# Convolution and ELU layer on one core: x cast once per super through a DRAM copy, convolutions moved amid output rounds, loads reordered at the start

## Chip, cores, metric

One core of one Trainium2 chip. The metric is the device time of one execution in microseconds (us), lower is better. Executions of one kernel on one chip usually agree within a per cent (four of the kernel before: 850.81 to 853.84 us); a run more than 1.5% above the fastest of its kernel is called slow, the others fast. Ratios are computed as the mean time of one kernel's fast runs over that of the other's of the same rounds, so not quite the ratio of the medians quoted. Runs came from different chips, where the kernel before took 849 to 855 us; each run is therefore judged against the kernel before on its own chip.

## The reference

A softmax-weighted causal convolution over 7 tokens, 8 heads of 24 channels, then a two-layer network with ELU:

```python
# x (8, 4096, 192), weight (8, 7), w_in (192, 2048), w_out (2048, 192), all float32
w = softmax(weight, axis=-1)
att[b, s, h*24 + c] = sum_k w[h, k] * x_padded[b, s + k, h*24 + c]   # 6 zero rows in front
h = att.reshape(32768, 192) @ w_in
g = where(h > 0, h, exp(min(h, 0)) - 1)
out = g @ w_out                                                      # (32768, 192) float32
```

## The kernel before

The 32,768 tokens are worked off in 32 *supers* of 1,024. A super has 16 *steps*; in each, a pair of 64-row slices of h goes round a loop of four engines through one of three PSUM slots `H`:

```python
# TensorE (PE): 12 matmuls fill H[slot]; then 9 or 10 "output rounds" of g @ w_out
# ScalarE (ACT):   E = exp(H[slot])                         (2 x 512 columns)
# GpSimd (POOL):   E = max(min(E, 1), 0)                    "clamp"
# VectorE (DVE):   g = max(E - 1, H[slot])                  frees the slot
```

The convolution is also done by PE, in two parts per super, each of which takes one of the three slots; ScalarE evacuates it to `csb`, and it goes through DRAM (`conv_slots`) into `att` with another layout. x is cast from float32 to bfloat16 on its way into `xg`, in overlapping windows of 122 rows, and GpSimd issues these loads between its clamps:

```python
CONV_AT = ((7, 2, 0), (15, 2, 1))   # (step, supers ahead, part): after the rounds of steps 7 and 15
X_AT = (1, 5, 13)                   # steps at which GpSimd issues the x loads
...
for n in range(NP):                 # GpSimd's loop
    s, i = divmod(n, NQ)
    if i in X_AT and s + NXB < NS:
        load_x(s + NXB, X_AT.index(i))      # part 0: only where a batch begins; parts 1, 2: windows
    for u in range(2):
        W(s_exp, 2 * n + u + 1)
        g.tensor_scalar(out=E[:, n % NE, u, :], ..., op0=ALU.min, op1=ALU.max).then_inc(s_clp)
...
if n in rounds_at:                  # PE's order of work
    order.append(("o",) + rounds_at[n])
for at, ahead, g in CONV_AT:
    if i == at and s + ahead < NS and n < NP:
        conv_at(s + ahead, g)
```

After 64 output rounds the output is evacuated (`osb<-ops`, L271) twice per super, at steps 2 and 10. The distance between two such evacuations is called a *half* below; it is the pulse by which the text measures the loop.

## Time and profile before

| | before |
|---|---|
| median, three runs | 852.95 us |
| first output evacuation | 66.73 us |
| half, steady | 12.44 us |
| busy: PE, GpSimd, ScalarE, VectorE | 89, 78, 77, 76% |

The first and fourth parts of the page of the kernel before: busy time of each engine, and the chain of work that ended last, by engine. PEld is PE's loading of weights, which overlaps its matmuls (752.5 and 560.4 us of busy time in a span of 849.9).

```profile
PE 752.5 (89%) x25088; PEld 560.4 (66%) x25088; DVE 643.3 (76%) x1031; ACT 650.5 (77%) x1156; POOL 662.8 (78%) x1115
...
PE 35%; POOL 26%; DVE 17%; ACT 9%; issue 9%; DMA 3%; SPq 0%; POOLq 0%; ACTq 0%
```

No engine is full, the chain is mixed, and the engines wait for each other in a ring (80 to 770 us: VectorE for GpSimd 134.2 us, GpSimd for ScalarE 122.6, ScalarE for PE 100.7, PE for VectorE 30.7): so I read that the loop's latency through three slots bounds it. The next fence is that chain in order of time (start, length, what), in one half of the kernel before.

```profile
409.35 2.35 POOL E L248 x4
411.70 0.73 POOL xg L198
412.43 0.03 issue
412.46 0.64 POOL E L248
413.10 0.02 issue
413.13 2.49 DVE gT L333 x4
415.62 0.14 issue
415.75 0.37 PE H L392
```

The GpSimd issue of an x load (L198) stands between clamps, and everything behind it waits. What a part costs can be read from the run itself, because the x loads stop first and the convolutions next. This is the busy time of each engine in three stretches of the kernel before, each from one evacuation to the next: with convolution and x load, with convolution alone, with neither.

```profile
core 0: us, PE busy (x) PEld busy (x) DVE busy (x) ACT busy (x) POOL busy (x), PEclk, DMA share, GB/s
420.49:432.93 12.44, 11.64 (x400) 8.50 (x392) 10.09 (x17) 10.17 (x20) 10.24 (x18) 1.00 0.54 134
785.38:797.10 11.72, 11.63 (x396) 9.18 (x392) 10.01 (x17) 10.00 (x20) 9.46 (x17) 1.00 0.20 61
819.30:830.10 10.80, 10.78 (x360) 7.97 (x352) 10.01 (x17) 9.07 (x18) 9.45 (x17) 1.00 0.13 41
```

These are the lines of the waits of the kernel before that have PE waiting for *issue*, that is, for nothing the profile shows, between 80 and 770 us (total us, times, longest), and the line of the DMA queues that carries instructions.

```profile
PE ops L414 <- issue: 4.6, 4, 1.7
PE H L370 <- issue: 1.6, 1, 1.6
PE H L392 <- issue: 0.6, 1, 0.6
```

```profile
q8 instruction: 196, 3.21, 1.6%
```

The three waits sum to 6.8 us. The sum of these three lines is called *issue waits* below. The queue line says that instructions are fetched during the run: 196 packets, 3.21 MB. Each packet has 16,384 bytes in the trace's records. PE ran 25,088 matmuls and 25,088 weight loads (and 71 semaphore and drain instructions), 50,176 in all without the 71, which is 256 for each of the 196 packets. So I take these packets to be essentially PE's program (an estimate from these counts), one about every 4 us (3.98 in the median between 80 and 770 us).

### The profile page before, as it was taken

The page shows a single profiled execution, that of the slowest core. Times are in us where ns is not written, and L with a number is a line of the kernel's source. Part 1 is how long each engine was busy: PE and PEld are TensorE (multiplying, and loading weights), DVE is VectorE, ACT ScalarE, POOL GpSimd, SP SyncE. Part 2 cuts the span into 40 slices and gives each one's busy share as a digit, 9 for nine tenths or more (in the row PEclk, how much of TensorE's full clock was granted, in tenths as well). Part 3 has the DMA queues.
Part 4 walks back from the last instruction along what each step waited for, and adds up shares of the span by engine and source line. Part 5 has one row for each costly group of instructions (what it writes and reads, how often), then busy time and mean ns, then how long its engine had stood idle before and what let it go on. Part 6 is the DMA issues. An engine that isn't in the chain of part 4 may idle for free.

```text
span 849.9 us, 54707 instructions
## 1 busy us (share of the span) xinstructions
PE 752.5 (89%) x25088; PEld 560.4 (66%) x25088; DVE 643.3 (76%) x1031; ACT 650.5 (77%) x1156; POOL 662.8 (78%) x1115
## 2 busy tenths in 40 slices
PE   0279999889999999989999989999999999999997
PEld 0147667667766666766766766767766766677776
DVE  1277878777878878778777877878787887888894
ACT  1278888778878878878888868888787887888884
POOL 3378888778788788878788868788778878877883
PEclk9999999999999999999999999999999999999999
DMA  7774453444453444444335444344445434443211
GB/s 121 131 148 114 105 121 94 94 99 111 106 123 90 109 94 110 115 106 111 102 80 117 112 101 110 96 93 112 106 106 122 100 91 103 111 115 94 91 41 59
DMA packets 109190, 88.51 MB, mean 104 GB/s; under 512 B 46432, under 2 KB 95584, under 8 KB 108896
## 3 DMA queue, kind: packets, MB, share of 16 engines
q1 hardware_dynamic: 68016, 69.30, 26.1%
q0 software_dynamic: 40944, 15.72, 17.1%
q8 instruction: 196, 3.21, 1.6%
q14 instruction: 34, 0.28, 0.1%
HBM read 56.89 MB, written 42.24 MB: 117 GB/s over the span
## 4 chain that ended last, share of the span: by engine, by line
PE 35%; POOL 26%; DVE 17%; ACT 9%; issue 9%; DMA 3%; SPq 0%; POOLq 0%; ACTq 0%
POOL E L248 20%; PE H L392 19%; DVE gT L333 17%; PE ops L414 16%; ACT E L294 6%; POOL xg L198 5%; ACT osb L271 3%; DMA conv_slots<-csb 1%; DMA conv_band<-wprb 1%; DMA att<-conv_slots 1%; PE H L370 1%; DMA Tm<-conv_band 0%; SPq L475 0%; DMA wq<-in_weight_dram 0%; ACT csb L283 0%
## 5 line engine op out<-in xcount | busy, mean ns | idle before, releaser
L333 DVE SCALAR_TENSOR_TENSOR gT<-E,H 128x512 f16<-128x512 f32 x1024 | 640.0, 682 | 191.0 <-POOL E L248 182.1
L248 POOL TENSOR_SCALAR E<-E 128x512 f32<-128x512 f32 x1024 | 602.4, 614 | 148.1 <-ACT E L294 142.7
L294 ACT ACTIVATE E<-H 128x512 f32<-128x512 f32 x1024 | 546.6, 605 | 138.4 <-PE H L392 138.1
L392 PE MATMUL H<-att,w_in 64*64 64x512 bf16 x6144 | 429.7, 381 | 57.7 <-DVE gT L333 38.3
L414 PEld LDWEIGHTS ops<-w_out,gT 64*64 64x64 f16 x16384 | 377.9, 107 | 90.1 <-issue 9.5
L414 PE MATMUL ops<-w_out,gT 64*64 64x192 f16 x16384 | 422.5, 243 | 7.5 <-issue 6.4
L392 PEld LDWEIGHTS H<-att,w_in 64*64 64x64 bf16 x6144 | 165.9, 107 | 154.2 <-DVE gT L333 63.5
L283 ACT ACTIVATE csb<-H 128x1024 bf16<-128x1024 f32 x64 | 65.5, 1024 | 47.1 <-PE H L370 47.1
L370 PE MATMUL H<-Tm,xg 128*24 128x122 bf16 (+1 forms) x2560 | 43.2, 212 | 28.3 <-DMA Tm<-conv_band 15.2
L370 PEld LDWEIGHTS H<-Tm,xg 128*24 128x24 bf16 x2560 | 33.9, 93 | 41.2 <-DMA Tm<-conv_band 15.2
L198 POOL DMA_DIRECT2D xg<-in_x_dram x64 | 53.0, 830 | 10.2 <-DMA Tm<-conv_band 10.2
L271 ACT ACTIVATE osb<-ops 128x768 f32<-128x768 f32 x64 | 52.3, 817 | 8.4 <-PE ops L414 8.4
L235 POOL DMA_DIRECT2D w_out<-in_moe_w_out_dram x1 | 1.1, 1102 | 15.4 <-DMA att<-conv_slots 15.4
L207 POOL DMA_DIRECT2D xg<-in_x_dram x8 | 4.8, 604 | 0.3 <-issue 0.3
L217 POOL DMA_DIRECT2D w_in<-in_moe_w_in_dram x6 | 3.5, 606 | 0.3 <-PE H L370 0.3
L206 POOL MEMSET xg<- 6x192 bf16 x8 | 2.0, 247 | 0.3 <-POOLq L512 0.3
L326 DVE MEMSET H<- 128x2048 f32 x1 | 1.8, 1765 | 0.4 <-issue 0.4
L307 DVE TENSOR_REDUCE wmx<-wq 128x8 f32<-128x56 f32 x1 | 0.2, 213 | 2.2 <-DMA wq<-in_weight_dram 2.2
L260 ACT ACT_TABLE_LOAD x1 | 1.3, 1283 | 0.7 <-PEq L512 0.7
L264 ACT ACTIVATE wex<-wq 128x56 f32<-128x56 f32 x1 | 0.2, 249 | 1.7 <-DVE wq L309 1.7
L305 DVE MEMSET Tm<- 128x544 uint32 x1 | 0.5, 512 | 0.9 <-PEq L512 0.9
L316 DVE TENSOR_REDUCE wsum<-wex 128x8 f32<-128x56 f32 x1 | 0.2, 211 | 0.3 <-ACT wex L264 0.3
(9 smaller groups left out, 1.5 us busy)
## 6 DMA issues: line engine op xcount, KB each, us to landing
att<-conv_slots SPq DMA_DIRECT2D x192, 128.0 KB
out_dram<-osb SPq DMA_DIRECT2D x128, 192.0 KB, 3.3
conv_slots<-csb SPq DMA_DIRECT2D x64, 256.0 KB, 2.2
xg<-in_x_dram POOLq DMA_DIRECT2D x40, 192.0 KB, 3.7
xg<-in_x_dram POOLq DMA_DIRECT2D x24, 240.0 KB, 5.3
w_in<-in_moe_w_in_dram POOLq DMA_DIRECT2D x6, 128.0 KB, 5.6
w_in<-w_in SPq DMA_DIRECT2D x2, 384.0 KB, 5.3
w_out<-in_moe_w_out_dram POOLq DMA_DIRECT2D x1, 768.0 KB, 8.4
```

What stands on the lines that cost most here:

```text
L198: g.dma_start(xg[:, s % NXB, w0:w1, :], src).then_inc(s_x[s % NXB], 16)
L206: g.memset(xg[0:PAD, b, 0, :], 0.0).then_inc(s_z)
L207: g.dma_start(xg[PAD:P, b, 0, :], x_flat[t0 : t0 + P - PAD, :]).then_inc(s_x[b], 16)
L217: g.dma_start(w_in[0:HP, j, FH * k : FH * (k + 1)], bass.AP(tensor=moe_w_in.tensor, offset=8 * j * FF + FH * k, ap=[[CPH * FF, HEADS], [FF ...
L248: g.tensor_scalar(out=E[:, n % NE, u, :], in0=E[:, n % NE, u, :], scalar1=1.0, scalar2=0.0, op0=ALU.min, op1=ALU.max,).then_inc(s_clp)
L271: a.activation(osb[:, b, :, :, :].rearrange("p g k d -> p g (k d)"), ops[:, :, 0 : 2 * D], ACT.Copy,).then_inc(s_oev)
L283: a.activation(csb[:, m % 4, :, :], H[:, slot_of_conv[m] % 3, :].rearrange("p (b t) -> p b t", b=2), ACT.Copy,).then_inc(s_ce)
L294: a.activation(E[:, n % NE, u, :], H[:, k, GS * u : GS * (u + 1)], ACT.Exp).then_inc(s_exp)
L333: v.scalar_tensor_tensor(out=gT[:, s % NG3, 2 * q + u, :], in0=E[:, n % NE, u, :], scalar=1.0, in1=H[:, slot_of_pair[n] % 3, GS * u : GS * ...
L370: ins = pe.matmul(H[SLOT * q : SLOT * q + CPH, k % 3, GS * hb + o : GS * hb + o + nc_], xg[:, s % NXB, w, CPH * h : CPH * (h + 1)], Tm[:, ...
L392: ins = pe.matmul(H[HP * c : HP * (c + 1), k % 3, GS * r : GS * (r + 1)], w_in[HP * r : HP * (r + 1), j, HP * f : HP * (f + 1)], att[HP * ...
L414: ins = pe.matmul(ops[HP * c : HP * (c + 1), g, D * kb : D * (kb + 1)], gT[HP * g : HP * (g + 1), t % NG3, f, t0 : t0 + HP], w_out[HP * g ...
```

## The change

Its intent: leave GpSimd one DMA per super. GpSimd casts a whole super of x into a padded DRAM copy, four supers ahead; the windows are then plain loads from that copy, issued by SP. Convolutions go into the middle of the output rounds at steps 0 and 8. At the start, later loads are held back until the first `att` has landed, the att reads are shared between two queues, and idle matmuls are meant to keep PE's clock up.

```diff
+QA = 10
+WARM = (20, 18)
-CONV_AT = ((7, 2, 0), (15, 2, 1))
-X_AT = (1, 5, 13)
+CONV_AT = ((0, 2, 0), (8, 2, 1))
+EARLY_CONV = {5: (1, 0), 7: (1, 1), 11: (2, 0), 14: (2, 1)}
+CAST_AT, CAST_AHEAD = 2, 4
+LOAD_AT, LOAD_AHEAD = 4, 3
 ...                                                     # PE's order of work
+            t, half, r0, r1 = rounds_at[n]
+            mid = (r0 + r1) // 2 if convs else r1
+            order.append(("o", t, half, r0, mid))
+            for k, g in convs:
+                conv_at(k, g)
+            if mid < r1:
+                order.append(("o", t, half, mid, r1))
 ...                                                     # GpSimd, before its loop
             load_w_in(0)                                # now after the diagonal write
-            W(s_cv, 2)
+            W(s_att[0], 16 * NDMA_ATT)
+            if NS > 1:
+                load_x(1)
             load_w_in(1)
             ... w_out ...
+            if NS > 2:
+                load_x(2)
 ...                                                     # GpSimd's loop
-                if i in X_AT and s + NXB < NS:
-                    load_x(s + NXB, X_AT.index(i))
+                if i == CAST_AT and s + CAST_AHEAD < NS:
+                    k = s + CAST_AHEAD
+                    b, row = k // SPB, PAD + k % SPB * SUP
+                    g.dma_start(
+                        xpad[b, row : row + SUP, :].rearrange("(p k) d -> p (k d)", p=P),
+                        x_flat[k * SUP : (k + 1) * SUP, :].rearrange(
+                            "(p k) d -> p (k d)", p=P
+                        ),
+                    ).then_inc(s_xc[k % CAST_AHEAD], 16)
 ...                                                     # PE
+            warm(WARM[0])
 ...                                                     # the second warm-up, ScalarE's att reads
 ...                                                     # SP
-                    if s == 0:
-                        copy_w(1)
-                        copy_w(2)
+                    if m == 1:
+                        read_att(sy, W, 0, (0,))
+                        ...
+                        copy_w(1)
+                    elif m == 3:
+                        read_att(sy, W, 1, (0, 1))
+                        copy_w(2)
+                elif item[0] == "h":
+                    s, i = divmod(item[1], NQ)
+                    if i == 1 and s >= 1 and s + 1 < NS:
+                        W(s_h, NQ * s)
+                        read_att(sy, W, s + 1, (0, 1))
+                    k = s + LOAD_AHEAD
+                    if i == LOAD_AT and CAST_AHEAD <= k < NS:
+                        ...                              # waits for the casts
+                        x_windows(sy, xpad, k, 0, XW, row, s_xh)
+                        x_windows(sy, xpad, k, XW, NWIN, ..., s_xh)
```

More of the change, by code (lines that the diff above doesn't have):

```diff
@@ L102, in bass_lightweight_conv__then__act_elu_kernel @@
             order.append(("h", n))
-        if n in rounds_at:
-            order.append(("o",) + rounds_at[n])
-        for at, ahead, g in CONV_AT:
-            if i == at and s + ahead < NS and n < NP:
-                conv_at(s + ahead, g)
-        if n in (3, 5) and NS > 1:
-            conv_at(1, (3, 5).index(n))
+        if s == 0:
+            convs = [EARLY_CONV[n]] if n in EARLY_CONV else []
+        else:
+            convs = [(s + ahead, g) for at, ahead, g in CONV_AT if at == i and n < NP]
+        convs = [(k, g) for k, g in convs if k < NS]
+        if n in rounds_at:
+            t, half, r0, r1 = rounds_at[n]
[5 more added lines that the diff above has]
+                order.append(("o", t, half, mid, r1))
+        else:
+            for k, g in convs:
+                conv_at(k, g)
+    xpad = nc.dram_tensor("x_padded", (Bsz, PAD + S, D), BF16).ap()
     band = nc.dram_tensor("conv_band", (P, HEADS, TW), BF16).ap()
@@ L140, in bass_lightweight_conv__then__act_elu_kernel @@
         wprb = sbuf("wprb", [P, HEADS, KSIZE], BF16)
+        zrow = sbuf("zrow", [Bsz, PAD * D], BF16)
+        zw = sbuf("zw", [P, GS], BF16)
         scr = sbuf("scr", [P, 2], FP32)
@@ L152, in bass_lightweight_conv__then__act_elu_kernel @@
         s_z = sema("s_z")
+        s_zr = sema("s_zr")
+        s_zw = sema("s_zw")
+        s_zp = sema("s_zp")
+        s_xh = [sema(f"s_xh{i}") for i in range(NXB)]
+        s_xc = [sema(f"s_xc{i}") for i in range(CAST_AHEAD)]
         s_h = sema("s_h")
@@ L178, in __call__, with x_windows, read_att @@
                     self.eng.wait_ge(sem, value)
-        FH = FF // 2
+        WCOLS = ((0, P * QA), (P * QA, FF))
         NDMA_ATT = 6
-        x_need, x_count, z_count = {}, [0] * NXB, 0
+        x_need, x_count = {}, {}
         for s in range(NS):
-            x_count[s % NXB] += 32 + 16 * (s % SPB == 0)
-            z_count += s % SPB == 0
-            x_need[s] = (x_count[s % NXB], z_count)
+            sem = (s_x if s < CAST_AHEAD else s_xh)[s % NXB]
+            x_count[id(sem)] = x_count.get(id(sem), 0) + 32 + 16 * (s == 0)
+            x_need[s] = (sem, x_count[id(sem)])
+        def x_windows(eng, flat, s, w0, w1, row, sem):
+            src = bass.AP(
+                tensor=flat.tensor,
+                offset=row * D,
+                ap=[[D, P], [CW * D, w1 - w0], [1, D]],
+            )
+            eng.dma_start(xg[:, s % NXB, w0:w1, :], src).then_inc(sem[s % NXB], 16)
+        def read_att(eng, W, s, halves):
+            for m in (2 * s, 2 * s + 1):
+                W(s_dw[m % 4], 16 * (m // 4 + 1))
+            for r in halves:
+                for j in range(3):
+                    src = bass.AP(
+                        tensor=bounce.tensor,
+                        offset=(2 * P * (s % 2) + 8 * j) * SUP,
+                        ap=[[SLOT * SUP, HEADS], [SUP, 8], [1, SUP]],
+                    )
+                    eng.dma_start(
+                        att[HP * r : HP * (r + 1), s % 2, j, :, :].rearrange(
+                            "p g t -> p (g t)"
+                        ),
+                        src,
+                    ).then_inc(s_att[s % 2], 16)
         @block.gpsimd
@@ L190, in _gpsimd, with load_x @@
             W = Waits(g)
-            def x_windows(s, w0, w1, row):
-                src = bass.AP(
-                    tensor=x_flat.tensor,
-                    offset=row * D,
-                    ap=[[D, P], [CW * D, w1 - w0], [1, D]],
-                )
-                g.dma_start(xg[:, s % NXB, w0:w1, :], src).then_inc(s_x[s % NXB], 16)
-            def load_x(s, part):
+            def load_x(s):
                 b, t0 = s % NXB, s * SUP
-                first = s % SPB == 0
                 if s >= NXB:
                     W(s_cv, 2 * (s - NXB) + 2)
-                if part == 0 and first:
+                if s == 0:
                     g.memset(xg[0:PAD, b, 0, :], 0.0).then_inc(s_z)
@@ L209, in load_x @@
                     ).then_inc(s_x[b], 16)
-                elif part == 1:
-                    x_windows(s, int(first), XW, t0 - PAD + CW * first)
-                elif part == 2:
-                    x_windows(s, XW, NWIN, t0 + SUP - P - CW * (NWIN - 1 - XW))
+                w0 = int(s == 0)
+                x_windows(g, x_flat, s, w0, XW, t0 - PAD + CW * w0, s_x)
+                x_windows(g, x_flat, s, XW, NWIN, t0 + SUP - P - CW * (NWIN - 1 - XW), s_x)
             def load_w_in(k):
+                c0, c1 = WCOLS[k]
                 for j in range(3):
                     g.dma_start(
-                        w_in[0:HP, j, FH * k : FH * (k + 1)],
+                        w_in[0:HP, j, c0:c1],
                         bass.AP(
                             tensor=moe_w_in.tensor,
-                            offset=8 * j * FF + FH * k,
-                            ap=[[CPH * FF, HEADS], [FF, 8], [1, FH]],
+                            offset=8 * j * FF + c0,
+                            ap=[[CPH * FF, HEADS], [FF, 8], [1, c1 - c0]],
                         ),
                     ).then_inc(s_w[k], 16)
-            for part in range(3):
-                load_x(0, part)
+            load_x(0)
+            g.memset(zrow[:], 0.0).then_inc(s_zr)
+            W(s_band, 32)
             load_w_in(0)
-            W(s_band, 48)
-            for part in range(3):
-                load_x(1, part)
-            W(s_cv, 2)
+            W(s_att[0], 16 * NDMA_ATT)
+            if NS > 1:
+                load_x(1)
             load_w_in(1)
-            W(s_att[0], 16 * NDMA_ATT)
             g.dma_start(
@@ L238, in _gpsimd @@
             ).then_inc(s_w[2], 16)
-            for s in range(2, min(NXB, NS)):
-                for part in range(3):
-                    load_x(s, part)
+            if NS > 2:
+                load_x(2)
             for n in range(NP):
                 s, i = divmod(n, NQ)
-                if i in X_AT and s + NXB < NS:
-                    load_x(s + NXB, X_AT.index(i))
+                if i == CAST_AT and s + CAST_AHEAD < NS:
[5 more added lines that the diff above has]
+                            "(p k) d -> p (k d)", p=P
+                        ),
+                    ).then_inc(s_xc[k % CAST_AHEAD], 16)
+                if n == LOAD_AT and NS > NXB:
+                    load_x(NXB)
                 for u in range(2):
@@ L287, in _scalar @@
                     ).then_inc(s_ce)
+                    if m == 1:
+                        read_att(a, W, 0, (1,))
                 elif item[0] == "h":
@@ L304, in _vector @@
             W = Waits(v)
+            v.memset(zw[:], 0.0).then_inc(s_zw)
             v.memset(Tm[:], 0.0).then_inc(s_tz)
@@ L353, in wait_slot, with warm @@
                     W(s_ce, was[1] + 1)
+            def warm(count):
+                W(s_zw, 1)
+                for _ in range(count):
+                    pe.matmul(ops[:, 0, :], zw[:, 0:P], zw[:], start=True, stop=True)
+            warm(WARM[0])
             for item in order:
@@ L361, in _tensor @@
                         W(s_hz, 1)
-                    W(s_x[s % NXB], x_need[s][0])
-                    W(s_z, x_need[s][1])
+                    W(*x_need[s])
+                    W(s_z, 1)
                     k = slot_of_conv[m]
@@ L382, in _tensor @@
                     s, q = divmod(n, NQ)
-                    W(s_w[q // 8], 48)
-                    W(s_wd[q // 8], 16)
+                    if n == 0:
+                        warm(WARM[1])
+                    W(s_w[q // QA], 48)
+                    W(s_wd[q // QA], 16)
                     W(s_att[s % 2], 16 * NDMA_ATT * (s // 2 + 1))
@@ L446, in copy_w @@
                 W(s_w[k], 16 if k == 2 else 48)
-                t = w_out if k == 2 else w_in[:, :, FH * k : FH * (k + 1)]
+                t = w_out if k == 2 else w_in[:, :, WCOLS[k][0] : WCOLS[k][1]]
                 sy.dma_start(t[HP:P, :, :], t[0:HP, :, :]).then_inc(s_wd[k], 16)
@@ L455, in _sync @@
                     W(s_ce, m + 1)
-                    if s >= 2:
-                        W(s_att[s % 2], 16 * NDMA_ATT * (s // 2))
                     sy.dma_start(
@@ L461, in _sync @@
                     ).then_inc(s_dw[m % 4], 16)
-                    if g == 0:
-                        continue
-                    for k in range(m - 1, m + 1):
-                        W(s_dw[k % 4], 16 * (k // 4 + 1))
-                    if s >= 2:
-                        W(s_h, NQ * (s - 1))
-                    for j in range(3):
-                        src = bass.AP(
-                            tensor=bounce.tensor,
-                            offset=(2 * P * (s % 2) + 8 * j) * SUP,
-                            ap=[[SLOT * SUP, HEADS], [SUP, 8], [1, SUP]],
-                        )
-                        for r in range(2):
-                            sy.dma_start(
-                                att[HP * r : HP * (r + 1), s % 2, j, :, :].rearrange(
-                                    "p g t -> p (g t)"
-                                ),
-                                src,
-                            ).then_inc(s_att[s % 2], 16)
@@ L481, in _sync @@
-                    if s == 0:
-                        copy_w(1)
-                        copy_w(2)
+                    if m == 1:
+                        read_att(sy, W, 0, (0,))
+                        W(s_zr, 1)
+                        sy.dma_start(
+                            xpad[1:Bsz, 0:PAD, :].rearrange("b r d -> b (r d)"),
+                            zrow[1:Bsz, :],
+                        ).then_inc(s_zp, 16)
+                        copy_w(1)
[9 more added lines that the diff above has]
+                    if i == LOAD_AT and CAST_AHEAD <= k < NS:
+                        W(s_zp, 16)
+                        for c in range(max(k - 1, CAST_AHEAD), k + 1):
+                            W(s_xc[c % CAST_AHEAD], 16 * (c // CAST_AHEAD))
+                        W(s_cv, 2 * (k - NXB) + 2)
+                        row = k // SPB * (PAD + S) + k % SPB * SUP
+                        x_windows(sy, xpad, k, 0, XW, row, s_xh)
+                        x_windows(
+                            sy, xpad, k, XW, NWIN,
+                            row + PAD + SUP - P - CW * (NWIN - 1 - XW), s_xh,
+                        )
```

## The prediction

> **What bounds it now.** A super (1024 tokens, 16 pair steps) is a loop through three PSUM slots: PE fills H, ScalarE exponentiates, GpSimd clamps, VectorE combines and frees the slot. No engine is full (page: PE 89% busy, GpSimd 78%, ScalarE 77%, VectorE 76%). The chain of waits is mixed: PE 35%, GpSimd 26%, VectorE 17%; 5% are GpSimd's issues of x loads (L198).
>
> The timeline prices each part, because x loads and convolutions stop before the end. Between successive output evacuations (L271), half a super:
>
> - 420.49 to 432.93 us, convolution and x load: 12.44
> - 785.38 to 797.10 us, convolution only: 11.72
> - 819.30 to 830.10 us, neither: 10.80
>
> So an x-load issue costs 0.72 us per half, nearly all of its 0.80 us; a convolution 0.92. The chain shows how: four clamps, the issue, a clamp, four VectorE operations, then the H matmul that waited for a slot.
>
> **What the change does.**
>
> 1. The cast leaves GpSimd one DMA per super instead of two, or three with a memset when a batch begins. [...] the trace agrees that the issue grows with pieces (0.60 us for w_in rows, 0.80 for windows, 1.10 for w_out). The cast has 128 long rows: I estimate 0.6 us. At step 2 it precedes an evacuation that delays the next exponentials anyway, so I count 0.1 to 0.3 us. Saved: 2 x 0.72 - 0.2 = about 1.2 us per super, over some 28 supers 34 us. Batch-start extras: 2 us.
> 2. Convolution amid output rounds still takes one of three slots, so VectorE still idles about 1.05 us behind it (as at 794.72). Nearly nothing: -0.15 to +0.2 us per half.
> 3. Windows come through SP from DRAM, 12 steps ahead. DMA share is about 45%; no new wait.
> 4. Start. The first H is at 34.45 us: the diagonal write takes 6.7 us, the conv writes about 7 beside other loads (2.2 in steady state), and six att reads are issued in a row at 0.65 us each. Holding loads back and splitting these reads should bring it to about 28 us. But GpSimd then issues x, w_in, w_out, x before its first clamp: 2 x 0.85 + 3 x 0.6 + 1.1 + 2 x 0.85 = 6.3 us against 2.8. Warm-up matmuls save at most 1.9 us (the first three pairs took 3.5 us, half the later pace). Net: 4 us.
> 5. PE's instruction-issue gaps (0.6 to 1.7 us), the last two supers and the tail stay.
>
> Sum: 853 - 34 - 2 - 4 = 813; I put 815[...]. Range 800 to 834. Chances: faster by over 2% (below 836) 0.85, within 2% 0.13, slower 0.02.
>
> **What would show it.** Halves near 11.7 us; one GpSimd DMA of about 0.6 us per super, x issues below 2% of the chain; VectorE's gap behind a convolution still about 1 us; GpSimd about 35 us less busy; first H near 28 us, first clamp near 34.
>
> **What would make it wrong.** The cast issue may be dearer, or stall the loop at step 2. Convolution and evacuation, now two steps apart instead of three, may queue on ScalarE (1.02 + 0.82 us): halves then near 12.1. If amid-round convolutions hide fully, halves fall to 11.3 and the time below 800. Extra DRAM traffic could lengthen PE's gaps. GpSimd's queue at the start may eat the startup gain.

The terms of the sum are 853 - 34 - 2 - 4 = 813 us, and 815 was forecast. That the issue grows with pieces is read from the page of the kernel before: 0.606 us for 64 rows of w_in, 0.830 for the 512 or 640 pieces of an x window load, 1.102 for the 2,048 pieces of w_out. The 1.9 us of the warm-up matmuls is an estimate from the first 36 matmuls (34.45 to 37.98 us); that idle matmuls would bring them to the later pace was assumed.

## The result

The changed kernel took 879.17 us (median of four runs, 878.80 to 883.08), the kernel before 852.89: ratio 1.032, 95% interval 1.029 to 1.036. It was slower, outside the predicted range on the wrong side.

| | before | after |
|---|---|---|
| median | 852.89 us | 879.17 us |
| first output evacuation | 66.73 us | 80.40 us |
| first to sixty-second evacuation | 763.4 us | 776.8 us |
| half from step 10 to 2, mean of supers 8 to 27 | 12.45 us | 11.86 us |
| half from step 2 to 10, mean of supers 8 to 27 | 12.75 us | 14.03 us |
| issue waits of PE, 80 to 770 us | 6.8 us | 50.4 us |

So the 27.5 us by which the profiled spans differ (849.9 and 877.4) are two losses of the same size: 13.7 us before the first evacuation, and 13.4 us after it, where 36 us had been expected as a gain. The same lines of the page, after:

```profile
PE 778.7 (89%) x25125; PEld 575.9 (66%) x25126; DVE 645.3 (74%) x1032; ACT 648.5 (74%) x1156; POOL 631.3 (72%) x1074
...
PE 78%; issue 8%; DMA 4%; POOL 3%; DVE 3%; ACT 3%; SPq 1%; ACTq 0%; POOLq 0%
```

GpSimd is 31.5 us less busy and nearly gone from the chain, as intended; the chain is PE's now. Two successive halves of the kernel after, in the table of stretches:

```profile
core 0: us, PE busy (x) PEld busy (x) DVE busy (x) ACT busy (x) POOL busy (x), PEclk, DMA share, GB/s
660.49:672.14 11.65, 11.55 (x400) 8.55 (x392) 9.84 (x16) 9.99 (x19) 9.67 (x18) 1.00 0.23 66
672.14:686.53 14.39, 12.12 (x399) 8.82 (x392) 9.95 (x17) 10.09 (x20) 9.70 (x17) 1.00 0.59 159
```

The first, from step 10 to step 2, is what was predicted: 11.65 us. The second has the same work, done at full clock, and takes 2.74 us longer; it is the half just behind the cast (issued at 671.52 us), with 159 GB/s of DMA. The timeline of PE in it, kernel after (start, length, engine, line, out<-in, count, idle time before it and what ended that):

```profile
681.23 0.61 PE L469 MATMUL ops<-w_out,gT 64*64 64x192 f16 x20
681.67 0.81 PE L447 MATMUL H<-att,w_in 64*64 64x512 bf16 x10
683.72 0.40 PE L447 MATMUL H<-att,w_in 64*64 64x512 bf16 x2 [1.25 <-issue]
683.73 0.97 PE L469 MATMUL ops<-w_out,gT 64*64 64x192 f16 x32
```

PE stops in the middle of a group of twelve matmuls that has no wait in it: after ten it stands for 1.25 us, then goes on. No semaphore of the program is involved. A wait of 0.98 us before 678.88 us is of the same kind; together they are 2.2 of the 2.74 us. The waits view of the kernel after, 80 to 770 us, answers to the one shown of before:

```profile
PE ops L469 <- issue: 32.0, 38, 2.8
PE H L447 <- issue: 11.3, 15, 1.6
PE H L423 <- issue: 7.1, 6, 3.5
```

50.4 us where there were 6.8. The instruction queue's own line has not changed:

```profile
q8 instruction: 196, 3.21, 1.6%
```

But the starts of these 196 fetches have. From the trace's records (what follows is computed from the packets' start and landing times and from PE's instruction starts): in the kernel before, successive fetches start about 3.4 to 4.9 us apart; in the kernel after, 15 of 164 gaps in the steady part are above 5.5 us (4 of 168 before), and most lie over a cast. Count the instructions that PE has started (semaphore and drain instructions too) by the time a fetch has landed, and subtract 256 for each fetch that had landed before it: the difference comes up to 448 and no further, in either kernel. Between 80 and 770 us, 21 fetches of the kernel after land within 8 instructions of that limit, 3 of the kernel before; 20 of the 21 and all 3 are followed by an issue wait of PE. So I read the limit as the point at which PE has nothing left to start.

The same records tie the waits themselves to the fetches. Number PE's instructions by their start, these too: all 59 issue waits of the kernel after (80 to 770 us) stand at the same place modulo 256, and all 6 of the kernel before at that place or one beside it. It is also the place at which the count above stops (448 is 256 + 192, and the waits stand at the matmul behind that weight load). I call it the start of a block. The last fetch had landed 1.25 to 1.60 us before the wait ended in the kernel after, 1.42 in the median. By the same count none of the other runs has an issue wait anywhere else. So I read the issue waits as waits for instructions, and estimate from these 59 that here a fetch is late already when it lands less than about 1.4 us before PE needs it; the fetches at the limit are the worst of them (28.5 of the 50.4 us).

The loss at the start is another wait. The chain in order of time, kernel after:

```profile
55.55 0.57 SPq L227
56.13 0.04 issue
56.17 10.91 DMA w_out<-w_out
67.08 0.14 issue
67.22 1.81 PE ops L469 x39
```

w_out's copy to the upper 64 partitions is issued by SP only after six att reads of the next super. It is needed for the first output round, and PE stood 10.4 us for it. In the kernel before SP issued this copy at 43.00 us. The first H did come earlier, at 29.58 us instead of 34.45.

The idle matmuls did not keep the clock up; that they would was assumed, and no run shows it. These are the rows of PE's granted clock in the two pages, in 40 slices of the span and tenths of full speed, before and after:

```profile
PEclk9999999999999999999999999999999999999999
PEclk9678999999999999999999999999999999999999
```

By the clock records of the traces, PE had half its clock for 37.5 of the first 80 us in the kernel after, for 3.4 in the kernel before (23.9 in e3 and e5 below, which keep the idle matmuls). No run took apart what that cost. Between 80 and 770 us it was 6.8 us against 3.4, too little to explain the steady loss.

### The profile page after: what moved, and what is told of

It is laid out like the page before. It is cut to its first block, busy times and chain, and to the rows that moved or that the text cites. A ratio compares the mean times of both kernels' runs of the same rounds, so it can differ in the third digit from the quotient of the medians.

```text
span 877.4 us, 54775 instructions
## 1 busy us (share of the span) xinstructions
PE 778.7 (89%) x25125; PEld 575.9 (66%) x25126; DVE 645.3 (74%) x1032; ACT 648.5 (74%) x1156; POOL 631.3 (72%) x1074
## 4 chain that ended last, share of the span: by engine, by line
PE 78%; issue 8%; DMA 4%; POOL 3%; DVE 3%; ACT 3%; SPq 1%; ACTq 0%; POOLq 0%
PE ops L469 37%; PE H L447 36%; PE H L423 4%; DVE gT L380 3%; POOL E L292 2%; ACT E L340 2%; DMA w_out<-w_out 1%; DMA conv_slots<-csb 1%; ACT osb L315 1%; POOL xg L215 1%; DMA w_in<-in_moe_w_in_dram 1%; DMA att<-conv_slots 1%; DMA conv_band<-wprb 1%; SPq L227 0%; DMA wq<-in_weight_dram 0%
## 5 line engine op out<-in xcount | busy, mean ns | idle before, releaser
L469 PE MATMUL ops<-w_out,gT 64*64 64x192 f16 x16384 | 451.3, 244 | 45.1 <-issue 33.0
L469 PEld LDWEIGHTS ops<-w_out,gT 64*64 64x64 f16 x16384 | 383.1, 107 | 140.6 <-issue 58.8
L447 PE MATMUL H<-att,w_in 64*64 64x512 bf16 x6144 | 436.4, 385 | 34.9 <-issue 11.6
L447 PEld LDWEIGHTS H<-att,w_in 64*64 64x64 bf16 x6144 | 176.3, 108 | 123.0 <-DVE gT L380 41.3
L215 POOL DMA_DIRECT2D xg<-in_x_dram x8 | 6.7, 845 | 17.8 <-DMA att<-conv_slots 17.8
L282 POOL DMA_DIRECT2D x_padded<-in_x_dram x28 | 15.0, 535 | 0.0
L405 PE MATMUL ops<-zw 128*128 128x512 bf16 x37 | 11.8, 492 | 1.5 <-DVE zw L351 1.2
L405 PEld LDWEIGHTS ops<-zw 128*128 128x128 bf16 x38 | 4.5, 122 | 8.1 <-issue 5.1
```

Of the source, the lines that this page charges most:

```text
L215: eng.dma_start(xg[:, s % NXB, w0:w1, :], src).then_inc(sem[s % NXB], 16)
L282: g.dma_start(xpad[b, row : row + SUP, :].rearrange("(p k) d -> p (k d)", p=P), x_flat[k * SUP : (k + 1) * SUP, :].rearrange("(p k) d -> p ...
L405: pe.matmul(ops[:, 0, :], zw[:, 0:P], zw[:], start=True, stop=True)
L447: ins = pe.matmul(H[HP * c : HP * (c + 1), k % 3, GS * r : GS * (r + 1)], w_in[HP * r : HP * (r + 1), j, HP * f : HP * (f + 1)], att[HP * ...
L469: ins = pe.matmul(ops[HP * c : HP * (c + 1), g, D * kb : D * (kb + 1)], gT[HP * g : HP * (g + 1), t % NG3, f, t0 : t0 + HP], w_out[HP * g ...
```

## The experiments

The theory after these views: **the cast's work on the DMA engines delays PE's instruction fetches**, and w_out's copy comes too late. Rivals: the convolution's new place; the volume of traffic bunched in steps 1 to 5; DRAM itself; the extra issue on GpSimd. The theories in the expectations below are guesses put to the test; what a run showed of them stands under each. In this table the issue waits are those of the three PE lines, 80 to 770 us, the halves are means of supers 8 to 27, and *starved* counts fetches at the limit. These four columns come from one profiled execution of each run: the slowest of the four for e3, e5, e11, e12 and e16, the fastest for e10 and e14. Differences of a few microseconds there are no evidence. Ratios are to the kernel before on the same chip, fast runs only.

| run | base and edit | median us | ratio, 95% interval | issue waits | half 2 to 10 | half 10 to 2 | starved |
|---|---|---|---|---|---|---|---|
| before | | 852.89 | 1 | 6.8 | 12.75 | 12.45 | 3 |
| after | the change | 879.17 | 1.032 (1.029 to 1.036) | 50.4 | 14.03 | 11.86 | 21 |
| e1_rows | after, cast in short rows | 890.20 | 1.041 (1.034 to 1.048) | 50.9 | 14.33 | 11.87 | 20 |
| e2_move | after, cast at step 11 | 897.28 | 1.046 (1.042 to 1.051) | 59.5 | 12.39 | 13.99 | 22 |
| e3_wout | after, w_out copy earlier | 875.90 | 1.023 (1.019 to 1.028) | 57.1 | 14.23 | 11.90 | 26 |
| e4_beforecast | before + cast to DRAM | 887.51 | 1.034 (1.028 to 1.040) | 42.0 | 14.27 | 12.56 | 20 |
| e5_direct | e3, direct x loads, no cast to DRAM | 846.99 | 0.995 (0.988 to 1.002) | 35.9 | 13.00 | 12.17 | 13 |
| e7_halves | e3, cast in 2 DMAs | 856.02 | none | 36.2 | 13.33 | 12.13 | 12 |
| e8_quarters | e3, cast in 4 DMAs | 853.64 | 1.001 (0.995 to 1.007) | 32.4 | 12.90 | 12.37 | 9 |
| e9_fourcasts | e3, casts end after super 3 | 836.49 | 0.979 (0.971 to 0.988) | 19.9 (190 to 770) | 12.70 | 11.92 | 5 (190 to 770) |
| e10_sbufcast | before + cast SBUF to SBUF | 882.08 | 1.034 (1.029 to 1.039) | 25.2 | 13.53 | 12.56 | 11 |
| e11_spread | e5, att reads one per step | 841.27 | 0.988 (0.983 to 0.992) | 35.2 | 12.83 | 12.22 | 13 |
| e12_spreadcast | e7 at steps 1, 9, traffic spread | 854.70 | 1.004 (1.000 to 1.008) | 49.8 | 12.71 | 13.11 | 15 |
| e13_whole | e5, convolution after the rounds | 847.55 | 0.992 (0.987 to 0.998) | 37.7 | 13.03 | 12.11 | 13 |
| e14_plain | before + plain copy by SP | 882.92 | 1.034 (1.029 to 1.039) | 27.5 | 13.44 | 12.58 | 15 |
| e16_tiny | before + tiny cast | 855.87 | 1.001 (0.995 to 1.006) | 10.9 | 12.87 | 12.52 | 3 |

### Is it the size of the cast's pieces? (e1_rows)

```diff
-    xpad[b, row : row + SUP, :].rearrange("(p k) d -> p (k d)", p=P),
-    x_flat[k * SUP : (k + 1) * SUP, :].rearrange("(p k) d -> p (k d)", p=P),
+    xpad[b, row : row + SUP, :].rearrange("(k p) d -> p k d", p=P),
+    x_flat[k * SUP : (k + 1) * SUP, :].rearrange("(k p) d -> p k d", p=P),
```

> The changed kernel, with the cast to DRAM cut into rows of 192 elements instead of runs of eight rows; same step, same bytes. Theory A (packet size): the cast's 24,576-byte packets, about 2.3 us each, stand before PE's own instruction fetches, which start 2 to 3 us late after a cast; with small packets the fetches slip in between. Then PE's waits put down to issue in the steady part (51.6 us between 70 and 790 us, against 7.7 before) fall below 20 us, halves with a cast fall from about 13.5 to near 12.2 us, time 879 -> about 850. The cast's issue on GpSimd gets dearer, 0.54 -> about 1.2 us. Theory B (bunching: cast, att reads, outputs and window loads all fall between steps 1 and 5, volume alone delays the fetches): no change or slower, 875 to 890, issue waits stay above 40 us. Theory C (the convolution at step 8 is what costs): no change.

No improvement: 890.20 us, issue waits 50.9. The trace's records show the cast in pieces of 384 bytes and some 51 ns instead of 24,576 bytes and some 2.3 us. So theory A in its first form, that one long piece blocks the fetch, fell. The work of a whole cast did not shrink, though: 1,024 pieces instead of 16, which is 64 for each of 16 DMA engines if they are spread evenly, some 3.3 us (an estimate, 64 x 51 ns). The issue on GpSimd rose from 0.54 to 0.90 us.

### Does the loss go along with the cast? (e2_move)

```diff
-CAST_AT, CAST_AHEAD = 2, 4
+CAST_AT, CAST_AHEAD = 11, 4
```

> The changed kernel, with the cast issued at step 11 instead of 2, away from att reads and window loads, packets as large as before. Theory A: the starving goes along with the cast: issue waits stay at 35 us or more, now in the halves from step 10 to step 2, time 865 to 885. Theory B: issue waits fall below 20 us and time to about 850. Theory C: halves from step 2 to step 10 stay at 13 us and more.

It goes along. The halves from step 2 to 10 fall from 14.03 to 12.39 us, and those from 10 to 2 rise from 11.86 to 13.99. The time is above the expected range, 897.28 us; PE had half its clock for 30.7 us between 80 and 770 us, against 6.8 in the kernel after, which can be part of that. Neither the bunching in steps 1 to 5 nor the convolution at step 8 explains that.

### The start (e3_wout)

```diff
+    elif m == 2:
+        copy_w(2)
     elif m == 3:
         read_att(sy, W, 1, (0, 1))
-        copy_w(2)
```

> The changed kernel, with the copy of w_out to the upper partitions issued by SP after the third convolution write instead of after the fourth and its six att reads. Theory of the start: PE stood 10.4 us for that copy (56.17 to 67.08 us) before its first output round, so the first evacuation comes 8 to 12 us earlier than 80.4 us, and the time falls by the same, to about 868. Rival: the start is slow because GpSimd issues 6.3 us of loads before its first clamp and everything behind it is late anyway: gain below 4 us.

The first evacuation comes at 68.0 us instead of 80.4, 12.4 us earlier, about as expected. The ratio falls from 1.032 to 1.023, some 8 us (two chips), so a part was given back. The profile shows longer issue waits (57.1 us), but it is of the slowest run, 879.86 us. Even so the start gained nothing on the kernel before (66.73 us): GpSimd's first clamp comes at 35.98 us in the kernel after, 37.45 before, though H begins 4.9 us earlier: GpSimd issues its eight loads first, from 29.73 to 35.92 us.

### The cast alone, in the old schedule (e4_beforecast, e10_sbufcast)

```diff
 # the kernel before, GpSimd's loop
+if i == 2 and s + 4 < NS:
+    ...                                                  # the changed kernel's cast, not read by anyone
+    g.dma_start(xpad[...], x_flat[...]).then_inc(s_xc, 16)
```

> The kernel before, with the changed kernel's cast to DRAM added at step 2 of each super (its copy is not read). It measures the cast by itself under the old schedule. Theory A: PE's issue waits rise from about 8 us to 30 us or more, and the time from 853 to 880 or more, more than the 28 x 0.54 = 15 us that the issues can cost on GpSimd. Theory C (the cast is harmless, the new convolution place is not): at most 15 us slower, issue waits below 15 us.

Ratio 1.034, issue waits 42.0 us, and the loss is in the half with the cast (14.27 us against 12.75). The cast by itself costs the old kernel as much as the whole change did.

e10_sbufcast puts an SBUF-to-SBUF cast of the same shape there (`g.dma_start(small[:], big[:])`, 128 x 1,536 elements):

> The kernel before, with one cast DMA per super at step 2 as in the run that added the cast to it (same issuer, same 128 rows of 1,536 elements), but from SBUF to SBUF: no DRAM is touched, and nothing reads the copy. Theory Q (a fetch waits for its turn on the DMA engines behind the cast's work): slows like the DRAM cast, ratio 1.025 to 1.04, issue waits above 30 us. Theory H (DRAM reads and writes delay the fetch's own read of DRAM): at most what 28 GpSimd issues cost, ratio 1.00 to 1.015, issue waits below 15 us.

The same ratio, 1.034, without touching DRAM. So DRAM contention is not needed. The issue waits, 25.2 us, stayed below what theory Q expected. The profile is of the fastest run (877.27 us); in it, the time from the third to the fifty-ninth evacuation is 23.6 us longer than in the kernel before. PE's issue waits there rose by 19.0 us, while its waits for VectorE fell by 5.1.

### Work or issue? GpSimd and casting, or any transfer? (e16_tiny, e14_plain)

Both are the kernel before plus one DMA per super at step 2.

```diff
 # e16_tiny: GpSimd, casts 128 x 8 elements, SBUF to SBUF
+    g.dma_start(small[:], big[:]).then_inc(s_xc, 16)
 # e14_plain: SP, 128 x 1,536 float32, SBUF to SBUF, no cast
+    W(s_h, NQ * s + i)
+    sy.dma_start(small[:], big[:]).then_inc(s_xc, 16)
```

> The kernel before, with one tiny cast per super from GpSimd at step 2, 128 rows of 8 elements: the same issue, almost no work on the DMA engines. If the work is what costs: ratio 1.00 to 1.01, issue waits below 12 us, GpSimd issue about 0.5 us each. If the extra GpSimd issue in the loop is the cost: ratio 1.02 or more.

> The kernel before, with one plain copy per super, SBUF to SBUF, 128 rows of 6,144 bytes, no cast, issued by SP when step 2's second H is done. If any long transfer on the DMA engines delays the fetches: ratio 1.015 to 1.035, issue waits above 20 us. If only transfers that cast, or that GpSimd issues, do: ratio below 1.008, issue waits below 12 us.

The tiny cast costs nothing measurable (ratio 1.001, 0.995 to 1.006; issue 0.59 us each, as long as e10's), the plain copy 3.4%. So here neither the GpSimd issue nor the casting matters, but the work on the DMA engines. The waits view of the plain copy's run, 80 to 770 us:

```profile
PE ops L419 <- issue: 18.4, 20, 2.2
PE H L397 <- issue: 5.1, 7, 1.3
PE H L375 <- issue: 4.0, 3, 2.9
```

and of the tiny cast's:

```profile
PE ops L423 <- issue: 6.1, 10, 1.8
PE H L379 <- issue: 3.4, 4, 1.6
PE H L401 <- issue: 1.4, 3, 0.7
```

The delay itself can be seen in the starts of the instruction fetches. This table, computed from the trace's records, counts fetches by the time since the added DMA was issued, over 26 supers; if the DMA did nothing, and with fetches some 3.95 us apart, each half microsecond would hold about 26 x 0.5 / 3.95 = 3.3.

```
us since issue   0-0.5  0.5-1  1-1.5  1.5-2  2-2.5  2.5-3  3-3.5  3.5-4  4-4.5  4.5-5  5-5.5  5.5-6  6-7
after              2      3      4      2      0      0      1      4      4      5      6      3     2
e4_beforecast      2      7      0      1      0      0      0      4      5      6      5      2     4
e10_sbufcast       4      4      4      0      0      0      3      7      1      5      3      2     1
e14_plain          2      8      5      4      4      0      0      0      2      0      1      0    14
e16_tiny           4      6      2      0      4      3      2      1      4      6      2      2     5
```

Behind these long transfers (384 KB written by a cast, 768 KB by the plain copy) there is a stretch of 1 us (after) or 1.5 us (e4, e10, e14) in which no fetch starts; behind the tiny one the longest is one column, 0.5 us. I take it that a fetch due in that gap starts late: of the kernel after, 15 gaps between fetches are above 5.5 us, of the kernel before 4.

### What the change gives without the cast (e9_fourcasts)

```diff
-if i == CAST_AT and s + CAST_AHEAD < NS:
+if i == CAST_AT and s < CAST_AHEAD:
 ...
-row = k // SPB * (PAD + S) + k % SPB * SUP
+row = PAD + S + k % SPB * SUP               # supers 4 to 7 for all later ones
```

> Wrong result on purpose: changed kernel with the earlier w_out copy, casting only supers 4 to 7 during supers 0 to 3, and loading these again for all later ones; so from super 4 on the cast's bytes and issue are gone and all else stays. If the cast is the only cause: issue waits below 12 us from 190 us on, halves 11.7 to 12.1 in both positions there, time 825 to 840. If the window loads through SP or the convolution's place take part, halves from step 2 to step 10 stay above 12.4 and the time above 850.

836.49 us, ratio 0.979: against e3 (1.023) 4.4 points less, about 37 us, estimated across two chips. Halves from 10 to 2 are at 11.92 us, but those from 2 to 10 at 12.70, above the 11.7 to 12.1 that was expected. So the cast is the main part of the loss, not all of it; att reads, outputs and window loads still fall there.

### Shorter bursts (e7_halves, e8_quarters, e12_spreadcast)

```diff
 # e7: two DMAs of 512 rows, steps 2 and 10; e8: four of 256 rows, steps 2, 5, 10, 13
-    xpad[b, row : row + SUP, :] ... x_flat[k * SUP : (k + 1) * SUP, :]
+    xpad[b, row + j : row + j + 512, :] ... x_flat[k * SUP + j : k * SUP + j + 512, :]
```

> Changed kernel with the earlier w_out copy, and the cast in two DMAs of 512 rows at steps 2 and 10. Small packets (the first run of rows) did not help, so the revised theory A2 is: a fetch waits for the whole work that a cast has put on its DMA engine, some 3 us; [...] issue waits fall from 57 to below 20 us and time from 876 to about 850. Rival D (what counts is the total of bytes moved DRAM to DRAM, however spread): 870 to 885.

> As the run in halves, but four DMAs of 256 rows at steps 2, 5, 10 and 13. A2: [...] issue waits below 12 us; but GpSimd now issues four DMAs of about 0.5 us, so time 840 to 860. Rival D: 870 to 890.

Three of e7's four runs, and its profile, counted as slow (842.22 us fast, 855.81 to 856.59 slow), so e7 is not decided. Four DMAs gave 853.64 us, ratio 1.001 against e3's 1.023, although GpSimd spent 59.5 us on issues instead of 15.0. Issue waits fell to 32.4 us, not below 12. So spreading helps, less than A2 said, and rival D did not hold.

e12 moves the two halves to steps 1 and 9, the att reads to steps 2 to 7, one each, and the window loads to step 11:

> The changed kernel with the earlier w_out copy, the cast in two halves at steps 1 and 9 (GpSimd's gap behind a convolution), att reads one per step at 2 to 7, window loads at step 11. Burst theory: issue waits below 20 us, halves 11.7 to 12.3, ratio 0.97 to 0.985. Otherwise as the run in halves, about 1.0.

A miss: ratio 1.004, issue waits 49.8 us. By its issue waits, half a cast in each of two steps starved PE not much less than a whole one did (57.1 us in e3), though fewer fetches are at the limit (15 against 26) and the ratio is better than e3's 1.023. How long a burst may be is thus not settled.

### x loaded directly, and the convolution's place (e5_direct, e13_whole, e11_spread)

e5 keeps all of the change but the DRAM copy: GpSimd loads the windows itself again, at steps 1 and 9.

```diff
+X_AT = (1, 9)
 ...
-    if i == CAST_AT and s + CAST_AHEAD < NS: ...         # the cast, and SP's window loads
+    if s + NXB < NS:
+        for part, at in enumerate(X_AT):
+            if i == at:
+                load_x(s + NXB, (part,))
```

> The changed kernel with the earlier w_out copy, and with x loaded as before (cast by GpSimd straight into SBUF, no DRAM copy), its two window loads issued at steps 1 and 9, in the gap of about 1 us that GpSimd has behind a convolution. Everything of the change but the cast stays. If the cast's delay of PE's instruction fetches is what made the change slow, issue waits go back to about 8 us and halves to 11.7 to 12.1 us in both positions: 820 to 835 us. If the convolution amid output rounds or the new start are the cause, it stays above 853. If an x-load issue costs 0.72 us wherever it stands, halves are about 12.4 and the time about 850.

846.99 us, ratio 0.995: as fast as before, not the 820 to 835 hoped for. Undisturbed halves are at 11.65 us, so an x load behind a convolution costs nothing there, but the issue waits are still 35.9 us.

e13 sets `mid = r1`, the convolution after the rounds:

> The kernel with direct x loads at steps 1 and 9, with the convolution after the output rounds of steps 0 and 8, not amid them. My prediction held this neutral (-0.15 to +0.2 us per half): 840 to 858 us, ratio within 0.01 of the run with it amid. If the place amid the rounds is what brought the good halves from 12.44 to 11.65 us, it rises by 20 us or more.

847.55 us, ratio 0.992 (0.987 to 0.998) against e5's 0.995 (0.988 to 1.002): neutral, as the prediction had it.

e11 is e5 with the att reads one per step:

```diff
-    if i == 1 and s >= 1 and s + 1 < NS:
+    if i in ATT_AT and s >= 1 and s + 1 < NS:            # ATT_AT = (2, 3, 4, 5, 6, 7)
         W(s_h, NQ * s)
-        read_att(sy, W, s + 1, (0, 1))
+        k = ATT_AT.index(i)
+        read_att(sy, W, s + 1, (k % 2,), (k // 2,))
```

> The kernel with direct x loads at steps 1 and 9 (846.99 us, ratio 0.995), with its six att reads issued one per step at steps 2 to 7 instead of in a row at step 1. If bursts from any source delay the fetches, issue waits fall from 33 to below 15 us and the ratio to 0.965 to 0.98. If only the casting transfers do, nothing changes: 0.99 to 1.0.

841.27 us, ratio 0.988: the best correct version, but only 1.2% faster than the kernel before. Its issue waits did not fall (35.2 us, in the profile of its slowest run), so its small gain was not the one expected; the interval overlaps e5's.

## Why the prediction was wrong

**Right.** The price of an x load in the loop, and what it brings when it is gone: halves without disturbance are at 11.65 us, where 11.7 was predicted. The cast's issue takes 0.54 us (0.6 predicted), GpSimd is 31.5 us less busy (35), x issues are 1% of the chain (below 2). The convolution amid the rounds is neutral (e13). VectorE's gap behind it is 0.8 us in the kernel after (before the operation at 671.03 us), where 1 was predicted. First H at 29.58 us (28), first clamp at 35.98 (34).

**Wrong, the main step: "Windows come through SP from DRAM, 12 steps ahead. DMA share is about 45%; no new wait."** and with it "PE's instruction-issue gaps ... stay". They did not stay: issue waits went from 6.8 to 50.4 us. With it fails the cost that step 1 gave the cast, 0.1 to 0.3 us per super for its issue alone: the half behind the cast took 14.03 us, not 11.7. The DMA share is an average of a whole slice; what counted was that a fetch of PE's program that fell due behind the cast started late. The step was shown, not only argued: a transfer alone, in the old schedule, costs 3.4%, whether it casts or not, touches DRAM or not, is issued by GpSimd or SP (e4, e10, e14), a tiny one costs nothing (e16), the loss moves with the cast (e2), without later casts the changed kernel is at 0.979 (e9), and every issue wait stands where a newly fetched block begins. "Extra DRAM traffic could lengthen PE's gaps" stood among the risks, without a number, and named DRAM, which is not needed.

The page of the kernel before had the fetches (q8, 196 packets), and I gave them no weight.

A second effect can have made the kernel after more sensitive. At the median landing of a fetch PE still had about 130 instructions in hand in the kernel before, 84 in the kernel after (448 less the median of the count above; an estimate from the traces). 784 instructions take 12.44 us in one and 11.65 in the other, so that is about 2.1 and 1.2 us of reserve. By this estimate the faster loop leaves less in time, and 1.2 us is less than the 1.4 us that passed between a landing and the end of the wait for it. That fits the 35 us of issue waits in e5 and e11, which have no cast to DRAM, but no run took this effect apart from the other transfers.

**Wrong, the start: "Net: 4 us" gain.** It was 13.7 us lost. I read the order of GpSimd's loads but not SP's: w_out's copy behind the att reads of super 1 landed at 67.08 us. e3 took 12.4 us of that back.

**The sum.** 36 us predicted for the steady part, 13.4 lost: 49 us off, of which the cast accounts for about 37 (e3 against e9). The start: 4 predicted, 13.7 lost, 18 off.

**What stays open.** Which DMA engine a fetch runs on and when it was asked for are not in the trace, so why a fetch starts late is not seen; only that it does. How short a burst must be is not settled (e8 against e12). The remaining 20 to 36 us of issue waits without a cast to DRAM (e5, e9, e11) stand at the start of fetched blocks too, but are not assigned to single transfers, and e11 shows that spreading the att reads does not remove them.

## What to carry to other kernels

Here PE's program came in during the run (196 packets of 16,384 bytes), and 59 waits on nothing, 50.4 us, stood at one place modulo 256 of PE's instructions. In another kernel, look for PE waiting on nothing in the middle of a group, count the instruction queue's packets, and see whether they start late behind a long transfer. The DMA engines' share was about 45% in the kernel before, and one plain copy per super added to it still cost 3.4% (e14): when work is moved from a compute engine onto them, try the new transfer alone in the old kernel first, and beside it one with the same issue but almost no data. When loads are reordered at the start, follow every queue to the first consumer, also the queue that was not the point of the change.
